# Two changes of where loads are issued: later keys, values and queries on GpSimd's queue, and the first queries ahead of the key-value products

## The chip, the cores and the metric

The kernel runs on one core of one Trainium2 chip. The metric is the device time of one execution in microseconds (us). Three runs of the kernel before took 1547.57, 1551.84 and 1552.95 us; their median, 1551.84 us, is the time before.

A core has five engines with a queue of instructions each: PE (TensorE, matrix products and transposes), DVE (VectorE), ACT (ScalarE), POOL (GpSimd) and SP (SyncE). Each works through its own queue strictly in order. An instruction that waits for a semaphore holds up everything behind it on that engine. Transfers between the memory of the chip and the core's on-chip memory (DMAs) are issued from such a queue too, and then run on 16 DMA engines which all queues share.

## The reference

```python
def _attn_ref(q, k, v, g_norm):                 # 8 batches, 8 heads, 576 positions, 64 wide
    kv = np.einsum('bhsd,bhse->bhde', k, v)
    out = np.einsum('bhsd,bhde->bhse', q, kv)
    rms = np.sqrt(np.mean(out * out, axis=-1, keepdims=True) + 1e-06)
    return out / rms * g_norm

x = attn_out.transpose(0, 2, 1, 3).reshape(4608, 512)
h = x @ w_in1;  g = h * np.clip(h + 3.0, 0.0, 6.0) / 6.0;  x = g @ w_out1     # layer 0: 512 -> 2048 -> 512
h = x @ w_in2;  g = h * np.cos(h);                          y = g @ w_out2     # layer 1: 512 -> 2048 -> 512
```

The attention is linear: each head needs a 64x64 product of keys and values, and then every query row is multiplied by it and normalised. The weights arrive in 8-byte numbers; the kernel decodes them itself.

## The kernel before, in words

The 4608 rows are worked on in nine superblocks of 512 rows, of four chunks of 128 rows each. There are three stages.

The prologue computes the four attention chunks of superblock 0. Batch 0's keys and values come in four pairs of heads: `kv_load` (L380) fetches one pair, `kv_pair` (L393) multiplies keys by values on PE (ten products, the last two on the 64 left-over positions in the tile `tail`), and DVE copies the result into `kvbd`. `q_load` (L419) fetches the queries of a chunk; `chunk` (L426) turns them on PE (`pq`), ACT copies them (`qT` or `tmp`), PE multiplies them by `kvbd` (`po`), ACT and DVE normalise, PE turns the result back (`px`) and ACT writes it to `xr`.

Then superblock 0 goes through layer 0 in float32: for each of 16 blocks `f`, `plain_1` (product `h`, L1012) and `plain_2` (product `acc`, L1027). This stage needs the decoded weights `di` and `do` of block pair `f // 2`. A weight is fetched by `raw_load` (L200, tiles `ri` and `ro`, 1024 KB each) into one of three raw buffers, decoded by ACT (L245, and L258 for a sum of squares) and DVE (L247, L251, L254). A raw buffer is free again after L258.

The remaining superblocks of layer 0 (products at L835 and L654) and all of layer 1 (L835 and L707) run as float16 products. During layer 0 a generator, `attention`, works off the other attention chunks between those products: for each batch four `kv_pair`s, and chunks in between. There is a single buffer, `kv_buf`, for the keys and values of the later batches: the load of a pair can start only when PE has done the products of the pair before it, and the next `kv_pair` stands in PE's queue at a place that is fixed when the program is built.

All loads and stores of the kernel before are issued from SP's queue, in the order in which the scheduler places them. What fixes the order on PE, DVE and ACT is the scheduler that builds the program; it follows the order of the Python code, with priorities, and its own expectation of when data arrive.

The steps touched are `kv_load` and `q_load`, the loads ahead of the prologue (L924 to L943) and the order of the prologue's work (L944 to L954).

Of the kernel before, what the change touches and what calls it, by code (L numbers as in the profile page):

```python
# [55 lines left out]
def attention_moe_kernel(  # L56
# [12 lines left out]
    nc = tc.nc  # L69
# [6 lines left out]
    NP = H // 2  # L76
# [32 lines left out]
    def col(n=1, p=P):  # L109
        c = next_col[0]  # L110
        next_col[0] = c + n
        return cols[0:p, c:c + n]
# [3 lines left out]
    kv_buf = const.tile([P, 2, 2, 5, D], F32, name="kv_buf")  # L116
# [26 lines left out]
    def ps_scratch(name):  # L143
        tag = scratch[turn_of[0] % len(scratch)]
        turn_of[0] += 1
        return ps_m.tile([P, 512], F32, tag=tag, name=name, bufs=2 if tag == "t" else 1)


    def pow2_scale(mx, name, squares, res, at=None):


        pt = ps_scratch(f"pt_{name}")
        nc.tensor.transpose(out=pt[0:1, 0:P], in_=mx, identity=ident)
        m1 = col(p=1)
        nc.vector.tensor_reduce(
            out=m1, in_=pt[0:1, 0:P], axis=AX.X, op=ALU.max, apply_absolute_value=True
        )
        yield
        pb = ps_scratch(f"pb_{name}")
        nc.tensor.matmul(out=pb[:, 0:1], lhsT=ones_row, rhs=m1, start=True, stop=True)  # L160
        t = sm_p.tile([P, 1], F32, tag="sc", name=f"t_{name}")
        lo, hi = (2.0 ** -96, 2.0 ** 96) if squares else (2.0 ** -48, 2.0 ** 48)
        nc.vector.tensor_scalar(out=t, in0=pb[:, 0:1], scalar1=hi, scalar2=lo, op0=ALU.min, op1=ALU.max)
        pw = sm_p.tile([P, 1], U32, tag="pw", name=f"pw_{name}")
        if squares:
            nc.vector.tensor_scalar(
                out=pw, in0=t.bitcast(U32), scalar1=1, scalar2=0x3F800000,
                op0=ALU.logical_shift_right, op1=ALU.bitwise_and,
            )
        else:  # L170
            nc.vector.tensor_scalar(
                out=pw, in0=t.bitcast(U32), scalar1=0x7F800000, scalar2=None, op0=ALU.bitwise_and
            )
        s, inv = at or (col(), col())
        nc.vector.tensor_scalar(out=inv, in0=pw.bitcast(F32), scalar1=(2.0 ** 63 if squares else 1.0) / TOP, scalar2=None, op0=ALU.mult)
        nc.vector.reciprocal(out=s, in_=inv)
        res[name] = (s, inv)
        yield

    def tiny(name, a, b=None, imm=None):  # L180
        t = col()
        if b is not None:
            nc.vector.tensor_tensor(out=t, in0=a, in1=b, op=ALU.mult)
            a = t
        if imm is not None:
            nc.vector.tensor_scalar(out=t, in0=a, scalar1=imm, scalar2=None, op0=ALU.mult)
        return t
# [6 lines left out]
    scale = {}  # L194
# [182 lines left out]

    def kv_load(b, p, t=kv_buf, tail=True):  # L380
        for n, src in enumerate((k, v)):
            nc.sync.dma_start(
                out=t[:, n, :, 0:4, :].rearrange("p h c d -> p h (c d)"),
                in_=src[b, 2 * p:2 * p + 2, 0:512, :].rearrange("h (p c) d -> p h (c d)", c=4),
            )
            if tail:
                nc.sync.dma_start(
                    out=t[0:64, n, :, 4, :],
                    in_=src[b, 2 * p:2 * p + 2, 512:576, :].rearrange("h p d -> p h d"),
                )  # L390
        return t

    def kv_pair(b, p, t, tail=None):  # L393
        ps = ps_scratch(f"kv{b}_{p}")
        for c in range(5):
            for h in range(2):
                if c == 4 and tail is not None:
                    kh, vh = (tail[:, m, 2 * p + h] for m in range(2))
                else:
                    kh, vh = (t[:, m, h, c, :] for m in range(2))  # L400
                nc.tensor.matmul(
                    out=ps[64 * h:64 * h + 64, 0:64], lhsT=kh, rhs=vh, start=(c == 0), stop=(c == 4)
                )
        for h in range(2):
            r = slice(64 * h, 64 * h + 64)
            nc.vector.tensor_copy(out=kvbd[r, b % 2, p, r], in_=ps[r, 0:64])
        yield

    def parts(c):

        r, res = 0, []
        while r < P:
            b, s = divmod(c * P + r, S)
            n = min(P - r, S - s)
            res.append((b, s, r, n))
            r += n
        return res

    def q_load(c, t=None):  # L419
        if t is None:  # L420
            t = at_p.tile([P, H, D], F32, tag="q", name=f"q{c}")
        for b, s, r, n in parts(c):
            nc.sync.dma_start(out=t[r:r + n], in_=q[b, :, s:s + n, :].rearrange("h p d -> p h d"))
        return t

    def chunk(c, qt, dst, after=None, tmp=None):  # L426
# [451 lines left out]
    def run(gen):  # L878
        for _ in gen:
            pass  # L880

    def g_scale():
        yield from pow2_scale(gn, "g", False, scale)
        nc.vector.tensor_scalar(
            out=gs, in0=gn, scalar1=scale["g"][0], scalar2=0.125, op0=ALU.mult, op1=ALU.mult
        )
        yield
# [34 lines left out]
    kv_t = {}  # L922
    q_t = {}
    tail = wi_p.tile([P, 2, H, D], F32, tag="wi", name="tail")  # L924
    nc.gpsimd.memset(tail[64:P], 0.0)
    nc.gpsimd.memset(kv_buf[64:P, :, :, 4, :], 0.0)
    kv_t[0, 0] = kv_load(0, 0, tail=False)
    for n, src in enumerate((k, v)):
        nc.sync.dma_start(out=tail[0:64, n], in_=src[0, :, 512:576, :].rearrange("h p d -> p h d"))
    for p in range(1, NP):  # L930
        t = wi_p.tile([P, 2, 2, 5, D], F32, tag="wi", name=f"kvs{p}")
        kv_t[0, p] = kv_load(0, p, t, tail=False)
    for c in range(2):
        q_t[c] = q_load(c)
    free["s"] -= 2
    xr0 = [s_p.tile([P, 2, TT], F32, tag="s", name=f"xr0_{n}") for n in range(2)]
    start(weights())
# [2 lines left out]
    nc.sync.dma_start(out=gn[64:128, :], in_=g_norm.rearrange("(p o) -> p o", o=1))  # L940
    qs = wi_p.tile([P, 2, H, D], F32, tag="wi", name="qs")
    for c in range(2):
        q_t[2 + c] = q_load(2 + c, qs[:, c])  # L943
    for p in range(NP):  # L944
        run(kv_pair(0, p, kv_t.pop((0, p)), tail))
    run(g_scale())
    isx = tiny("isx", scale["g"][1], imm=8.0)
    pro = [
        chunk(
            c, q_t.pop(c), [(2 * n, xr0[n][:, :, c * P:(c + 1) * P]) for n in range(2)],  # L950
# [1 line left out]
        )  # L952
        for c in range(4)
    ]  # L954
    n = 0
    while pro:
        for g in list(pro):
# [19 lines left out]
    def attention():  # L977

        n_kv, n_task = NP, 0
        kv_t[kvs[n_kv]] = kv_load(*kvs[n_kv])  # L980
        for c in (4, 5):
            q_t[c] = q_load(c)
        for c in range(4, NC):
            while n_kv < len(kvs) and kvs[n_kv][0] <= parts(c)[-1][0]:
                yield from until(ATT0 + n_task * ATTR)
                yield from kv_pair(*kvs[n_kv], kv_t.pop(kvs[n_kv]))
                n_kv, n_task = n_kv + 1, n_task + 1
                if n_kv < len(kvs):
                    kv_t[kvs[n_kv]] = kv_load(*kvs[n_kv])
            yield from until(ATT0 + n_task * ATTR)  # L990
            j, n = divmod(c, 4)
            if n == 0:
                yield from take("raw")
                xr = raw_p.tile([P, KD, TT], F32, tag="raw", name=f"x{j}")

            def after(c=c):
                if c + 2 < NC:
                    q_t[c + 2] = q_load(c + 2)

            yield from take("at")  # L1000
            start(run_chunk(c, xr, after))
            yield
            n_task += 1
# [91 lines left out]
    n = NG * (NSB - 2)  # L1095
# [36 lines left out]
```

## Time and profile before

| | |
|---|---|
| median of three runs | 1551.84 us |
| the profiled execution, its time | 1551.0 us |
| its span, first to last instruction | 1549.1 us |
| PE busy | 1516.1 us (98%) |
| DVE busy | 1226.3 us (79%) |
| ACT busy | 1052.3 us (68%) |
| POOL busy | 2.0 us |
| mean granted TensorE clock | 0.998 of full speed |
| bytes moved by SP's DMA queue | 178.28 MB |

The profile lists, for each engine, how long it was busy in a stretch of time. TensorE's clock has two levels, 1.2 and 2.4 GHz; a granted clock of 1.00 means 2.4 GHz and 0.50 means 1.2 GHz. A timeline row gives the start, the length, the engine and line, output and input tiles, and in square brackets the idle time of the engine before it with what ended it. The chain of waits is followed back from the last instruction: each row names what the next one waited for. Of a DMA, the row's time is from its issue until the data had landed. SPq is SP's queue.

### The profile page before, as it was taken

What the parts mean: (1) busy time and instruction counts of PE and PEld (TensorE: products, weight loads), DVE (VectorE), ACT (ScalarE), POOL (GpSimd) and SP (SyncE); (2) the same over time, 40 slices, a digit from 0 to 9 for tenths busy, and PEclk for the clock granted to TensorE, in tenths of its full rate; (3) what the DMA queues carried; (4) which work ended last, traced back from release to release, by engine and by line L of the source; (5) the groups of instructions that cost most, each with busy time, mean ns of one, the idle gap of its engine ahead of it and who ended that gap; (6) DMA issues with size and microseconds to landing.
All of it is one profiled execution on the core that took longest, in us unless ns stands there. A gap on an engine that the chain in (4) does not pass through costs nothing.

```text
span 1549.1 us, 28806 instructions
## 1 busy us (share of the span) xinstructions
PE 1516.1 (98%) x11902; PEld 1153.8 (74%) x11902; DVE 1226.3 (79%) x2234; ACT 1052.3 (68%) x1714; POOL 2.0 (0%) x8
## 2 busy tenths in 40 slices
PE   6999999999999999999999999999999999999998
PEld 6444676666667676766666678888888888888887
DVE  4899877786877687876475799989898989889881
ACT  4567665665666565665455788888888887878771
POOL 0000000000000000000000000000000000000000
PEclk9999999999999999999999999999999999999999
DMA  7653433325243342402031233343342424333434
GB/s 205 202 165 95 123 102 110 103 81 165 69 150 98 88 129 74 150 25 79 1 103 48 96 110 117 129 142 116 139 142 105 157 91 155 117 132 123 147 111 155
DMA packets 112067, 180.12 MB, mean 116 GB/s; under 512 B 51008, under 2 KB 83776, under 8 KB 102720
## 3 DMA queue, kind: packets, MB, share of 16 engines
q1 hardware_dynamic: 111936, 178.28, 34.9%
q8 instruction: 93, 1.52, 0.4%
q14 instruction: 38, 0.31, 0.1%
HBM read 144.70 MB, written 33.55 MB: 115 GB/s over the span
## 4 chain that ended last, share of the span: by engine, by line
PE 51%; DVE 31%; ACT 12%; DMA 3%; issue 2%; SPq 1%; ACTq 0%
PE acc L654 18%; PE P L835 10%; DVE uA L587 5%; PE R L835 5%; DVE uA L592 4%; DVE gs_A L264 4%; DVE gs_S L264 4%; ACT uA L589 3%; PE h L1012 3%; PE Q L835 3%; PE acc L1027 3%; DVE c L851 2%; ACT uA L590 2%; PE po L449 2%; PE P L707 2%
## 5 line engine op out<-in xcount | busy, mean ns | idle before, releaser
L835 PEld LDWEIGHTS <-wi 128*128 128x128 f16 x5712 | 557.3, 98 | 108.7 <-issue 5.1
L654 PE MATMUL acc<-g,wo 128*128 128x512 f16 x1536 | 368.9, 379 | 0.4 <-ACT g L561 0.3
L654 PEld LDWEIGHTS <-wo 128*128 128x128 f16 x1536 | 148.8, 98 | 135.0 <-issue 1.7
L835 PE MATMUL P<-xoB,wi 128*128 128x256 f16 x1536 | 190.3, 273 | 1.6 <-ACT sn L847 1.5
L835 PE MATMUL P<-xoT,wi 128*128 128x256 f16 x1536 | 189.1, 273 | 0.5 <-ACT sn L847 0.2
L707 PEld LDWEIGHTS <-gs_A 128*128 128x128 f16 x1632 | 159.7, 98 | 20.4 <-issue 1.9
L847 ACT ACTIVATE sn<-P 128x512 f32<-128x512 f32 x204 | 119.2, 584 | 63.3 <-PE P L835 62.7
L707 PEld LDWEIGHTS <-gs_S 128*128 128x128 f16 x1392 | 136.1, 98 | 22.0 <-issue 6.2
L589 ACT ACTIVATE uA<-uA,cols 128x512 f32<-128x512 f32 x144 | 103.6, 720 | 62.3 <-DVE uA L587 60.9
L548 ACT ACTIVATE u<-c,cols 128x512 f32<-128x512 f32 x96 | 77.9, 812 | 82.2 <-DVE c L851 62.3
L707 PE MATMUL P<-wo,gs_S 128*128 128x256 f16 x888 | 114.6, 273 | 5.0 <-ACT kv_buf L726 5.0
L563 DVE TENSOR_TENSOR g<-u,g 128x512 f16<-128x512 f32 x128 | 87.5, 687 | 30.1 <-ACT g L561 29.1
L707 PE MATMUL P<-wo,gs_A 128*128 128x256 f16 x840 | 107.2, 273 | 1.6 <-ACT kv_buf L726 1.6
L561 ACT ACTIVATE g<-u 128x512 f16<-128x512 f32 x128 | 80.1, 628 | 37.5 <-DVE u L550 36.9
L550 DVE SCALAR_TENSOR_TENSOR u<-u,cols,c 128x512 f32<-128x512 f32 x96 | 71.9, 749 | 39.7 <-ACT u L548 39.4
L262 ACT ACTIVATE gs_A<-uA,cols 128x512 f16<-128x512 f32 x125 | 88.3, 713 | 16.2 <-DVE uA L592 11.3
L264 DVE SCALAR_TENSOR_TENSOR gs_A<-uA,cols,gs_A 128x512 f16<-128x512 f32 x125 | 92.6, 746 | 7.1 <-ACT gs_A L262 5.1
L585 ACT ACTIVATE uA<-c,cols 128x512 int32<-128x512 f32 x108 | 77.2, 715 | 30.0 <-DVE c L856 21.8
L835 PE MATMUL R<-xoT,wi 128*128 128x256 f16 x768 | 94.7, 273 | 0.0
L835 PE MATMUL Q<-xoB,wi 128*128 128x256 f16 x768 | 94.6, 273 | 0.0
L835 PE MATMUL R<-xoN,wi 128*128 128x256 f16 x768 | 94.5, 273 | 0.0
L592 DVE SCALAR_TENSOR_TENSOR uA<-uA,c 128x512 f32<-128x512 f32 x108 | 74.1, 686 | 23.0 <-ACT uA L590 22.1
(205 smaller groups left out, 2242.4 us busy)
## 6 DMA issues: line engine op xcount, KB each, us to landing
wo<-wod SPq DMA_DIRECT2D x63, 1024.0 KB, 4.9
ri<-in_moe_w_in_dram SPq DMA_DIRECT2D x16, 1024.0 KB, 6.5
ro<-in_moe_w_out_dram SPq DMA_DIRECT2D x16, 1024.0 KB, 5.1
x2d<-o SPq DMA_DIRECT2D x36, 256.0 KB, 2.5
xr<-x2d SPq DMA_DIRECT2D x9, 1024.0 KB, 4.8
out_dram<-o SPq DMA_DIRECT2D x36, 256.0 KB, 4.0
q<-in_q_dram SPq DMA_DIRECT2D x30, 256.0 KB, 2.9
kv_buf<-in_k_dram SPq DMA_DIRECT2D x29, 256.0 KB, 2.9
```

The source lines that it names most:

```text
L262: nc.scalar.activation(out=hi, in_=src, func=AF.Copy, scale=s)
L264: nc.vector.scalar_tensor_tensor(out=lo, in0=src, scalar=s, in1=hi, op0=ALU.mult, op1=ALU.subtract)
L548: nc.scalar.activation(out=u, in_=c, func=AF.Relu, scale=u0[:, gi:gi + 1], bias=b0[:, gi:gi + 1])
L561: nc.scalar.activation(out=gt[:, :, 0, sl], in_=u, func=AF.Copy)
L563: nc.vector.tensor_tensor(out=gt[:, :, 1, sl], in0=u, in1=gt[:, :, 0, sl], op=ALU.subtract)
L587: stt(out=u, in0=ui, scalar=nk, in1=c, op0=ALU.mult, op1=ALU.add)
L589: nc.scalar.activation(out=u, in_=u, func=AF.Sin, scale=hf)
L592: stt(out=u, in0=u, scalar=0.5 * SIG2, in1=c, op0=ALU.subtract, op1=ALU.mult)
L654: nc.tensor.matmul(out=acc[e], lhsT=w[:, a, row, e * P:(e + 1) * P], rhs=g[:, c], start=(n == 0 and i == 0), stop=(n == NF - 1 and i == 2),)
L707: nc.tensor.matmul(out=ps[:, mt], lhsT=g[:, c, pr, mt * P:(mt + 1) * P], rhs=w[:, i, a], start=(first and k == 0), stop=(end and k == 2), ...
L835: nc.tensor.matmul(out=ps[bank][:, pr], lhsT=w[:, a, A_AT[an], kk], rhs=x[:, c, kk], start=(first and pr == 0 and i == 0 and kk == 0), sto ...
L847: nc.scalar.activation(out=sn[n], in_=ps["P"], func=AF.Copy)
```

## The change

`kv_load` and `q_load` take the engine that issues their DMAs; without one it is GpSimd. The loads of the prologue (batch 0's keys and values, chunks 0 to 3's queries) name SP, so they stay on SP's queue. All later loads of keys, values and queries move to GpSimd's. Then the queries of chunks 0 and 1 are issued ahead of all keys and values, and the two generators that start chunks 0 and 1 are stepped once (the turn `pq` and the copy `tmp`) before the key-value products are written down.

```diff
-    def kv_load(b, p, t=kv_buf, tail=True):
+    def kv_load(b, p, t=kv_buf, tail=True, eng=None):
+        eng = eng or nc.gpsimd
         for n, src in enumerate((k, v)):
-            nc.sync.dma_start(
+            eng.dma_start(
...
-    def q_load(c, t=None):
+    def q_load(c, t=None, eng=None):
...
-            nc.sync.dma_start(out=t[r:r + n], in_=q[b, :, s:s + n, :].rearrange("h p d -> p h d"))
+            (eng or nc.gpsimd).dma_start(out=t[r:r + n], in_=q[b, :, s:s + n, :].rearrange("h p d -> p h d"))
...
-    kv_t[0, 0] = kv_load(0, 0, tail=False)
+    for c in range(2):
+        q_t[c] = q_load(c, eng=nc.sync)
+    kv_t[0, 0] = kv_load(0, 0, tail=False, eng=nc.sync)
...
-        kv_t[0, p] = kv_load(0, p, t, tail=False)
-    for c in range(2):
-        q_t[c] = q_load(c)
+        kv_t[0, p] = kv_load(0, p, t, tail=False, eng=nc.sync)
...
-        q_t[2 + c] = q_load(2 + c, qs[:, c])
-    for p in range(NP):
-        run(kv_pair(0, p, kv_t.pop((0, p)), tail))
-    run(g_scale())
-    isx = tiny("isx", scale["g"][1], imm=8.0)
+        q_t[2 + c] = q_load(2 + c, qs[:, c], nc.sync)
     pro = [
...
+    for g in pro[:2]:
+        next(g)
+    for p in range(NP):
+        run(kv_pair(0, p, kv_t.pop((0, p)), tail))
+    run(g_scale())
+    isx = tiny("isx", scale["g"][1], imm=8.0)
```

On SP's queue, the first place is right behind the first `ro` load of the prologue. `ri_0`, `ro_0` and `ri_1`, `ro_1` are the first two pairs of layer 0's weights; `kv_buf` rows are loads of batch 1's first two pairs, and `q_366`, `q_369` are chunks 4 and 5's queries. Before:

```order
17 L208 DMA ro_0_360<-in_moe_w_out_dram 128x2x1024
18 L382 DMA kv_buf<-in_k_dram 128x2x256
19 L387 DMA kv_buf<-in_k_dram 64x2x64
20 L382 DMA kv_buf<-in_v_dram 128x2x256
21 L387 DMA kv_buf<-in_v_dram 64x2x64
22 L423 DMA q_366<-in_q_dram 64x8x64 x2
23 L423 DMA q_369<-in_q_dram 128x8x64
24 L382 DMA kv_buf<-in_k_dram 128x2x256
25 L387 DMA kv_buf<-in_k_dram 64x2x64
26 L382 DMA kv_buf<-in_v_dram 128x2x256
27 L387 DMA kv_buf<-in_v_dram 64x2x64
28 L208 DMA ri_1_394<-in_moe_w_in_dram 128x4x512
```

The same stretch of SP's queue now, with the semaphores that each row waits for:

```order
13 L208 DMA ri_0_149<-in_moe_w_in_dram 128x4x512 [waits DMAHW4_49]
14 L940 DMA cols<-in_g_norm_dram 64x1 [waits DMAHW5_49]
15 L941 DMA cols<-in_g_norm_dram 64x1 [waits DMAHW6_49]
16 L424 DMA qs<-in_q_dram 128x8x64 [waits DMAHW7_49]
17 L424 DMA qs<-in_q_dram 128x8x64 [waits DMAHW0_49]
18 L208 DMA ro_0_360<-in_moe_w_out_dram 128x2x1024 [waits DMAHW1_49]
19 L208 DMA ri_1_394<-in_moe_w_in_dram 128x4x512 [waits DMAHW2_49]
20 L208 DMA ro_1_422<-in_moe_w_out_dram 128x2x1024 [waits DMAHW4_49,DMAHW3_49,Activation_49]
```

Eleven loads that stood between `ro_0` and `ri_1`, four of which wait for PE's products of batch 1's first pair, are gone from SP's queue.

On POOL's queue, whose only work was to fill tiles at the start, those loads now stand right behind that work, with these waits:

```order
10 L927 MEMSET kv_buf 64x4x64 [waits Pool_49]
11 L383 DMA kv_buf<-in_k_dram 128x2x256 [waits DMAHW2_49,PE_49]
12 L388 DMA kv_buf<-in_k_dram 64x2x64
13 L383 DMA kv_buf<-in_v_dram 128x2x256 [waits DMAHW3_49]
14 L388 DMA kv_buf<-in_v_dram 64x2x64
15 L424 DMA q_366<-in_q_dram 64x8x64 [waits DMAHW0_49,PE_49]
16 L424 DMA q_366<-in_q_dram 64x8x64
17 L424 DMA q_369<-in_q_dram 128x8x64 [waits DMAHW1_49,PE_49]
18 L383 DMA kv_buf<-in_k_dram 128x2x256 [waits DMASW0_49,PE_49]
```

The first of them waits only for the first loads of `kv_buf` and for the first eight products of batch 0; the queries wait for the turns of chunks 0 and 1.

On ACT the decode of the second pair of weights moves ahead of the work of blocks 0 and 1. Now:

```order
29 L482 ACTIVATE xr0_1_148<-px3_349,cols_116 128x2x128
30 L245 ACTIVATE di0_1_416<-ri0_1_394 128x1024
31 L245 ACTIVATE do0_1_444<-ro0_1_422 128x1024
32 L258 ACTIVATE ro0_0_360,cols_116<-do0_0_384 128x1024
33 L1021 ACTIVATE u0_0_413<-h0_0_396,cols_116 128x512
34 L1021 ACTIVATE u0_1_441<-h0_1_424,cols_116 128x512
```

Rows 30 and 31 stood behind row 34 before.

## Rows read from the trace of the kernel before

**Rows 1.** The page's first part: busy time, share of span, instructions.
```profile
PE 1516.1 (98%) x11902; PEld 1153.8 (74%) x11902; DVE 1226.3 (79%) x2234; ACT 1052.3 (68%) x1714; POOL 2.0 (0%) x8
```

**Rows 2.** Busy time in stretches: stretch, length, each engine, clock, DMA share, GB/s.
```profile
0.00:10.00 10.00, 2.95 (x40) 2.47 (x40) 1.75 (x6) 1.49 (x2) 1.97 (x8) 1.00 0.76 228
10.00:20.00 10.00, 8.43 (x71) 7.34 (x71) 3.15 (x11) 4.28 (x7) 0.00 (x0) 1.00 1.00 277
20.00:30.00 10.00, 6.31 (x37) 5.58 (x38) 8.71 (x35) 7.43 (x17) 0.00 (x0) 0.84 0.53 159
...
150.00:170.00 20.00, 19.20 (x126) 11.80 (x126) 19.92 (x45) 15.73 (x26) 0.00 (x0) 1.00 0.31 96
170.00:190.00 20.00, 18.68 (x172) 13.26 (x168) 16.06 (x31) 11.31 (x16) 0.00 (x0) 1.00 0.50 143
```

**Rows 3.** PE's timeline at the third block's first product.
```profile
46.88 5.37 PE L1012 MATMUL h<-xr,di 128*128 128x512 f32 x8 [2.25 <-DVE di L254]
```

**Rows 4.** The chain of waits, 31 to 74 us: start, length, what.
```profile
31.96 0.27 SPq L382
...
34.27 8.06 DMA ri<-in_moe_w_in_dram
42.35 1.14 ACT di L245
...
69.82 3.43 PE h L1012 x8
```

**Rows 5.** Stretches around PE's two idle times, columns as in rows 2.
```profile
24.00:26.00 2.00, 0.00 (x0) 0.00 (x0) 1.66 (x9) 1.83 (x4) 0.00 (x0) 1.00 0.67 150
...
28.00:29.00 1.00, 1.00 (x6) 1.00 (x6) 0.93 (x4) 0.80 (x3) 0.00 (x0) 0.50 0.00 0
...
48.00:49.00 1.00, 1.00 (x2) 0.34 (x1) 1.00 (x2) 1.00 (x1) 0.00 (x0) 0.50 0.00 0
```

**Rows 6.** The chain of waits in the prologue.
```profile
8.80 7.97 DMA ri<-in_moe_w_in_dram
16.80 1.15 ACT di L245
```

**Rows 7.** PE's timeline: the first key-value products.
```profile
4.42 1.12 PE L401 MATMUL kv<-kv_buf 128*64 128x64 f32 x16 [4.42 <-DMA kv_buf<-in_v_dram]
```

**Rows 8.** ACT's timeline: the instruction that frees the first raw buffer.
```profile
24.68 1.06 ACT L258 ACTIVATE ri<-di 128x1024 f32<-128x1024 f32 x1
```

**Rows 9.** PE's timeline around batch 2's key-value products.
```profile
163.70 0.80 PE L401 MATMUL kv<-kv_buf 128*64 128x64 f32 x20
...
168.16 0.27 PE L153 MATMUL pt_x<-ident,cols 128*1 128x128 f32 x1 [0.49 <-DVE cols L775]
...
169.49 0.80 PE L401 MATMUL kv<-kv_buf 128*64 128x64 f32 x20 [0.30 <-DMA kv_buf<-in_v_dram]
...
173.25 1.47 PE L835 MATMUL P<-xoB,wi 128*128 128x256 f16 x12 [0.69 <-ACT sn L847]
175.35 0.80 PE L401 MATMUL kv<-kv_buf 128*64 128x64 f32 x20 [0.63 <-DMA kv_buf<-in_v_dram]
...
182.86 0.80 PE L401 MATMUL kv<-kv_buf 128*64 128x64 f32 x20
```

**Rows 10.** The chain of waits: the load that ends the second wait.
```profile
172.13 3.08 DMA kv_buf<-in_v_dram
```

**Rows 11.** POOL's longest instruction, on its timeline.
```profile
1.00 0.95 POOL L925 MEMSET tail<- 64x1024 f32 x1
```

**Rows 12.** SP's queue: the longest issue of a left-over load in the prologue.
```profile
17.73 1.39 SPq L387 DMA_DIRECT2D kv_buf<-in_k_dram  x1
```

**Rows 13.** PE's timeline: two key-value products of batch 3, and layer 0's longest idle time.
```profile
244.94 0.80 PE L401 MATMUL kv<-kv_buf 128*64 128x64 f32 x20
254.24 0.80 PE L401 MATMUL kv<-kv_buf 128*64 128x64 f32 x20
...
270.34 0.38 PE L160 MATMUL pb_o<-cols,ones_row 1*128 1x1 f32 x2 [1.77 <-DVE cols L155]
```

More of the change, by code (lines that the diff above doesn't have):

```diff
@@ L386, in kv_load @@
             if tail:
-                nc.sync.dma_start(
+                eng.dma_start(
                     out=t[0:64, n, :, 4, :],
```

## The prediction

> **What bounds the kernel now.** I read the page's busy times first, then the busy time in stretches, then PE's timeline wherever PE was not full, and the chain of waits there. PE is busy for 1516.1 of 1549.1 us [rows 1], so all that any change of loads can win is in the 33 us in which PE stands still, and in stretches at the lower clock. In the stretches the reader is to see where those lie [rows 2]: 7.05 us in the first 10 us, 1.57 in the next ten, 3.69 in the third, and, much later, 0.80 and 1.32 us in the two stretches of 20 us in which batch 2's keys and values are multiplied. One more is on PE's timeline: 2.25 us ahead of the third block's product at 46.88 [rows 3]. Layer 1, more than half of the span, has no attention in it and none of the instructions that change.
>
> At the gap before 46.88 the chain of waits shows what ended last [rows 4]: weight `ri_1` was issued only at 34.27, because it stands in SP's queue behind the load of batch 1's second pair. That load needs `kv_buf`, which PE gave back only shortly before 31.96. The weight takes 8.06 us to land, then ACT and DVE decode it. When PE goes on it is slower: the granted clock is 0.50 (1.2 GHz) in the stretch from 48 to 49 us, and the same had happened from 28 to 29 us, after PE had stood still from 24 to 26 us [rows 5]. Eight `h` products then took 5.37 us [rows 3] where the same eight take 3.43 us later [rows 4].
>
> In the prologue the chain runs through `ri_0`: issued at 8.80, landed at 16.80, decoded by ACT at once [rows 6]. ACT's and DVE's decode of `ri_0` stand in their queues ahead of the evictions and sums of the attention chunks, before and after the change, so everything up to the first `h` is timed from that landing. DMA share is 1.00 from 10 to 20 us, at 277 GB/s [rows 2].
>
> **The change part by part.**
>
> *The gap at 46.88 goes.* `ri_1` now stands directly behind `ro_0` on SP's queue and has a free raw buffer, so it is issued as soon as `ro_0` is. `ro_1` needs the buffer that ACT's L258 frees at 24.68 + 1.06 = 25.74 [rows 8], well ahead of its use. The decode then stands right behind the last `xr` eviction. PE saves the idle 2.25 us and the slow clock's 5.37 - 3.43 = 1.94 us: -4.2 us. What is late next: in ACT's new order the decode of `do_1` stands ahead of `u0_0`, which PE waits for. `ri_1` took 8.06 us with other loads beside it [rows 4]; if `ro_1` takes as long it lands at about 34 us, when ACT gets to it. A few us more would cost PE about 1 us. I put 0, with 0 to 1 as bounds.
>
> *The prologue is held up.* Batch 1's first pair (256 + 32 + 256 + 32 KB) and chunk 4's queries (256 KB) stood behind `ro_0` in one queue. On POOL's they need only the first products and turns on PE: 4.42 + 1.12 [rows 7] and 1.9 us for the queries that now go first (512 KB at 277 GB/s), so from about 7.5 us, while `kvs`, `ri_0`, `qs` and `ro_0` are still to come on SP's queue. All of it goes through the same DMA engines, which are full. 832 KB at 277 GB/s is 3.1 us; chunk 5's 256 KB as well would make it 4.0, and if POOL's packets yielded to SP's it would be 0. I take 3.1: +3.1 us on `ri_0` and all behind it. The Trainium skill, "DMA: Bandwidth & Descriptors", section "Issuing engines are not separate DMA queues", says that DMAs run on the same 16 engines and interleave whichever engine started them, and that a second issuer only saves issue time. By that rule it is 3.1, and without it 0; the full share above agrees, but no row of this kernel has two queues at work.
>
> *The first queries ahead of the keys.* SP issues the same bytes ahead of `ri_0` in another order, so `ri_0` does not land sooner by it. The two turns and their two ACT copies go under the wait for keys and values. ACT had time for them in the trace too, since it starts the decode the moment that `ri_0` lands [rows 6]. I put 0. The key-value products come later by the same 1.9 us; `ri_0`'s landing covers that, and without the cover up to 1.9 would show.
>
> *Keys and values on POOL's queue in layer 0.* PE's place for each pair is fixed and `kv_buf` is single, so what counts is the time T from the end of one pair's products to the landing of the next pair. On SP's queue it was 172.13 + 3.08 - (169.49 + 0.80) = 4.9 us [rows 9, 10]. No row shows a DMA issued by POOL. From below, T stays 4.9. From above: four loads one after another at 1.39 us, the longest issue of such a load [rows 12], and the landing: 3 x 1.39 + 3.08 = 7.25 us. The nearest row on the engine itself is POOL's longest instruction, 0.95 us [rows 11]; with it T = 3 x 0.95 + 3.08 = 5.9 us, which I take. A sentence apart: the same page of the Trainium skill, table "Specifications", gives a first-byte latency of about 1 us for GpSimd's path and 0.6 for SP's; as an estimate that is 0.4 us for each of four loads in turn, T = 6.5 and 1.2 us more below.
>
> PE's other work between batch 2's first and second pair is 169.49 - 163.70 less 0.80 for the products and 0.49 and 0.30 of idle: 4.20 us; between second and third 5.86 - 0.80 - 0.69 - 0.63 = 3.74 [rows 9]. With T = 5.9 PE idles 1.7 and 2.2 us, 3.9 in place of the 2.1 that these two intervals idle now: +1.8. The third interval has 182.86 - 175.35 - 0.80 = 6.7 us of work and hides it. At T = 7.25 it is 3.05 + 3.5 + 0.55 - 2.1 = +5.0. Idles of this length may cost the clock too: 2.25 us was followed by 1.2 GHz [rows 3, 5], while no loss showed after 1.77 us [rows 13]. Each such fall is 1.9 us; I put none, and two (3.8) in the bound. In the later batches pairs are 254.24 - 244.94 = 9.3 us apart [rows 13], which leaves 8.5 us: hidden at any T up to there. Query loads have two chunks' time and are hidden. SP's other loads and stores lose the rows that stood in front of them; nothing on PE waited for those, so 0.
>
> *Sum.* 1551.0 (the profiled execution) - 4.2 + 3.1 + 1.8 = 1551.7. The median of the runs shown is 0.84 above the profiled execution, so 1552.5 us.
>
> **The rivals.**
>
> *POOL issues slowly (slower).* If POOL needs 1.39 us or more for each load, or has to wait for something it shares, T is 7.25 or more: -4.2 + 3.1 + 5.0 + 3.8 of clock = +7.7, about 1559.5 us. From T = 8.5 on it decides everything, since then 15 more intervals in batches 3 to 7 are exposed: at T = 10 these alone are 15 x 1.5 = 22 us, a time near 1590. For it: the chain is single-buffered and already waited for data on SP's queue twice [rows 9]. Against it: 15 of the 18 intervals of batches 2 to 7 have 8.5 us. DVE is busy for 19.92 of 20 us where the tight intervals lie [rows 2]. The Trainium skill, "SBUF — State Buffer", section "Who interferes with whom", says that GpSimd shares a pair of ports with DVE, and that it cannot write the descriptors of its DMAs while DVE works in a two-port mode. By that rule this rival is the likelier one the busier DVE is; no row of before shows POOL beside a busy DVE.
>
> *POOL's loads cost nothing (faster).* POOL starts late enough, or its packets are few enough in the full prologue, that `ri_0` lands as before, and T stays near 4.9. Then the 4.2 us stay won, and the weights decoded earlier can also take away the 0.49 and 0.69 us for which PE waited on DVE and ACT and part of 1.77 [rows 9, 13]: -4.2 to -7, about 1546.5. For it: DVE was busy for 19.92 of 20 us from 150 to 170 [rows 2], so earlier decoding could help there. Against it: the waits of the first POOL loads are over by about 7.5 us.
>
> *The gap is not removed.* `ri_1` is early, but `ro_1` or a later weight gates the in-order ACT queue, so PE stops at about the same place: +3.1 + 1.8 = about 1556.7. Against it: the raw buffers come free in time by the rows above.
>
> **How the numbers follow.** A change within 0.3% (4.7 us) is about what a measurement of this kernel can't tell from none. Forecast (gain and new waits nearly cancel) 0.46; POOL slow 0.30; POOL free 0.19; gap stays 0.05. Faster 0.20: nearly all of the free case, and a little of the forecast. Same 0.46. Slower 0.34. The likeliest case's own range, with 0 to 4.0 for the prologue, T up to 7.25 without the clock, is 1547.5 to 1557. The range that takes in the free case and the slow one up to T = 8.5 (4.0 in the prologue, 4.3 + 4.8 + 1.8 - 2.1 of idle, 3.8 of clock: 1564) is 1545 to 1565.
>
> **What would show it.** Right: PE's timeline has no idle of 2 us ahead of the third block's `h` and no 1.2 GHz stretch behind it; `ri_0` lands near 20 us in place of 16.8 and the first `h` starts about 3 us later; batch 2's second and third pairs wait about 2 us each for `kv_buf`; later batches wait for nothing. Wrong: `ri_0` lands by 17.5; POOL's queue shows issues of far over 1 us; PE waits for `kv_buf` in batches 3 to 7; a difference in layer 1.

## The result and the profile after

The changed kernel takes 1561.22 us (median of 4 runs, 1559.78 to 1563.57); the kernel before took 1550.63 in the runs beside it (4 runs, 1547.57 to 1552.95). The ratio is 1.0076, 95% interval 1.006 to 1.0091: slower, where the forecast was that no difference could be measured. The time lies in the range that was given, but outside the likeliest case's own. The profiled execution took 1561.49 us with a span of 1559.7 us, 10.6 us longer than before. A table of stages below shows where they lie in these two executions.

The page's busy times, queues (packets, MB, share of the 16 DMA engines' time) and DMA issues of the changed kernel (the issue rows end with size and median us to landing):

```profile
PE 1520.3 (97%) x11902; PEld 1156.7 (74%) x11902; DVE 1228.1 (79%) x2234; ACT 1053.2 (68%) x1714; POOL 105.9 (7%) x156
...
q1 hardware_dynamic: 55296, 153.37, 28.3%
q0 software_dynamic: 8896, 24.91, 5.5%
...
kv_buf<-in_k_dram POOLq DMA_DIRECT2D x28, 256.0 KB, 3.1
kv_buf<-in_v_dram POOLq DMA_DIRECT2D x28, 256.0 KB, 3.5
```

The same of the kernel before, where these loads were SP's:

```profile
q1 hardware_dynamic: 111936, 178.28, 34.9%
...
kv_buf<-in_k_dram SPq DMA_DIRECT2D x29, 256.0 KB, 2.9
kv_buf<-in_v_dram SPq DMA_DIRECT2D x29, 256.0 KB, 3.2
```

PE is busy 4.2 us longer than before [rows 1] with the same 11902 instructions: part of the loss is clock, the rest idle time. PE's timeline (start, length; in brackets idle time ahead and its releaser) shows both. `pt_g` is a small turn that belongs to the scale of `g_norm`, and `pb_o` and, further on, `pb_i` are small products that spread a weight's scale over the partitions. `o` is the tile in which a quarter of a superblock's result of layer 0 is stored to the array `x2d` in the chip's memory:

```profile
7.13 1.12 PE L402 MATMUL kv<-kv_buf 128*64 128x64 f32 x16 [7.13 <-DMA kv_buf<-in_v_dram]
...
19.72 0.27 PE L153 MATMUL pt_g<-ident,cols 128*1 128x128 f32 x1 [4.35 <-DMA cols<-in_g_norm_dram]
...
35.86 6.74 PE L1015 MATMUL h<-xr,di 128*128 128x128 f32 x58
42.44 3.60 PE L1030 MATMUL acc<-u,do 128*128 128x512 f32 x8
45.88 3.60 PE L1015 MATMUL h<-xr,di 128*128 128x512 f32 x8
...
163.19 0.80 PE L402 MATMUL kv<-kv_buf 128*64 128x64 f32 x20
...
172.06 1.33 PE L402 MATMUL kv<-kv_buf 128*64 128x64 f32 x20 [3.71 <-DMA kv_buf<-in_v_dram]
...
179.85 0.80 PE L402 MATMUL kv<-kv_buf 128*64 128x64 f32 x20
...
187.36 0.80 PE L402 MATMUL kv<-kv_buf 128*64 128x64 f32 x20
...
274.96 0.38 PE L160 MATMUL pb_o<-cols,ones_row 1*128 1x1 f32 x2 [1.88 <-DVE cols L155]
...
374.48 1.02 PE L655 MATMUL acc<-g,wo 128*128 128x512 f16 x3 [2.42 <-ACT o L668]
```

The gap ahead of the third block's `h` is gone, and the same eight products take 3.60 us where they took 5.37 [rows 3]. In return PE stands still in three other places: 4.35 us for the small load of `g_norm`, 3.71 us for batch 2's second pair (`kv2_1` in what follows), where it had waited 0.30 [rows 9], and 2.42 us at 374.48, where the kernel before shows no idle time at all. Behind each of them the granted clock falls (stretch, length, PE busy, clock, DMA share, GB/s):

```profile
20.00:24.00 4.00, 2.58 (x11) 0.50 0.98 351
...
172.00:176.00 4.00, 3.94 (x32) 0.50 0.45 149
276.00:280.00 4.00, 4.00 (x12) 0.58 0.13 50
374.00:378.00 4.00, 3.52 (x16) 0.62 0.19 71
```

The fourth, from 276 us, follows the 1.88 us wait of `pb_o`; the kernel before waited 1.77 us there [rows 13] and kept its clock. In the prologue the chain of waits shows the weight's landing at 19.29 in place of 16.80 [rows 6]:

```profile
8.12 11.15 DMA ri<-in_moe_w_in_dram
19.29 1.13 ACT di L245
```

POOL's own issues are short, also beside a busy DVE (2.92 of 3.00 us from 164 to 167). On POOL's timeline:

```profile
8.56 0.84 POOL L383 DMA_DIRECT2D kv_buf<-in_k_dram  x1 [5.86 <-PE kv L402]
...
164.18 0.70 POOL L383 DMA_DIRECT2D kv_buf<-in_k_dram  x1 [8.81 <-PE kv L402]
164.88 0.61 POOL L388 DMA_DIRECT2D kv_buf<-in_k_dram  x1
165.48 0.71 POOL L383 DMA_DIRECT2D kv_buf<-in_v_dram  x1
166.19 0.61 POOL L388 DMA_DIRECT2D kv_buf<-in_v_dram  x1
```

SP's queue shows what now runs beside them: a weight of 1 MB at 166.00 and another at 365.70, between two stores of `o`:

```profile
166.00 0.38 SPq L208 DMA_DIRECT2D ri<-in_moe_w_in_dram  x1
...
364.92 0.34 SPq L670 DMA_DIRECT2D x2d<-o  x1
365.70 0.38 SPq L208 DMA_DIRECT2D ro<-in_moe_w_out_dram  x1
366.96 0.32 SPq L670 DMA_DIRECT2D x2d<-o  x1
```

Before, that first weight was issued at 173.39, behind the loads of two pairs.

Cut at six instructions of PE that stand in the same order in every kernel here, each profiled execution gives a table of stages (us, from starts on PE's timeline):

| kernel | to first 58 `h` | to batch 2's first pair | to its fourth | to `pb_o` | to `pb_i` | to next `pb_o` | to end |
|---|---|---|---|---|---|---|---|
| before | 31.87 | 131.83 | 19.16 | 87.48 | 70.74 | 70.03 | 1137.99 |
| after | 35.86 | 127.33 | 24.17 | 87.60 | 72.27 | 74.04 | 1138.43 |
| difference | +4.0 | -4.5 | +5.0 | +0.1 | +1.5 | +4.0 | +0.4 |

The rounded differences add up to 10.5 of the 10.6 us. They are those of single executions: below, kernels whose prologues are the same differ by up to 1.5 us in the first stage.

### The profile page after: what moved, and what is told of

Read it like the earlier page. It is cut to its first block, busy times and chain, and to the rows that moved or that the text cites. A ratio compares the mean times of both kernels' runs of the same rounds, so it can differ in the third digit from the quotient of the medians.

```text
span 1559.7 us, 28841 instructions
## 1 busy us (share of the span) xinstructions
PE 1520.3 (97%) x11902; PEld 1156.7 (74%) x11902; DVE 1228.1 (79%) x2234; ACT 1053.2 (68%) x1714; POOL 105.9 (7%) x156
## 3 DMA queue, kind: packets, MB, share of 16 engines
q1 hardware_dynamic: 55296, 153.37, 28.3%
q0 software_dynamic: 8896, 24.91, 5.5%
## 4 chain that ended last, share of the span: by engine, by line
PE 46%; DVE 30%; ACT 12%; issue 8%; DMA 3%; POOL 1%; SPq 0%; POOLq 0%; ACTq 0%
PE acc L655 17%; PE P L836 10%; DVE uA L588 5%; PE R L836 5%; DVE uA L593 4%; DVE gs_A L264 4%; DVE gs_S L264 4%; ACT uA L590 3%; PE Q L836 3%; DVE c L852 2%; ACT uA L591 2%; PE h L1015 2%; PE P L708 2%; ACT gs_A L262 2%; PE acc L1030 2%
```

## The experiments

Three theories. T1, collision: SP's one queue had kept big weight loads away from transfers that PE or ACT waits for; with two queues they meet on the shared DMA engines, and each wait costs clock as well. T2: POOL's path is slow in itself. T3: the order with the queries first costs the time. Ratios below are against runs of the kernel before on the same chip, taken beside them.

**Each half of the change alone.** Only the loads moved, prologue order as before (all later batches' keys and values, and chunks from 4 on, on POOL):

```
+        eng = nc.sync if b == 0 else nc.gpsimd
...
-            nc.sync.dma_start(out=t[r:r + n], in_=q[b, :, s:s + n, :].rearrange("h p d -> p h d"))
+            (nc.sync if c < 4 else nc.gpsimd).dma_start(out=t[r:r + n], in_=q[b, :, s:s + n, :].rearrange("h p d -> p h d"))
```

> The kernel before with its order of the prologue, but with the later batches' keys, values and queries loaded by POOL. Three theories of the 10.6 us that the change lost. T1, collision: loads that no longer stand in one line on SP's queue run beside critical transfers: POOL's early loads beside ri_0 (+4.0 us), layer 1's weight ri_1 beside batch 2's keys and values (+5.0), ro_3 between the x2d stores (about +4), and the gap at the third block goes (-4.5). T2, POOL's path is slow in itself: its transfers take longer whatever runs beside them. T3, the queries-first order costs it. T1 and T2 expect 1559 to 1562 us here with the same three waits (kv2_1 on PE 3 to 4 us, o on PE near 374 us over 2 us, h of the first projection 3 to 4 us later than before); T3 expects about 1546 us, none of these.

Measured: 1558.47 us, ratio 1.0046 (1.0033 to 1.0058), half a microsecond under what T1 and T2 had. `kv2_1` waits 3.57 us, `o` lets PE wait 2.2 us, and the first 58 `h` begin at 35.58. And only the order, every load on SP:

```
-        eng = eng or nc.gpsimd
+        eng = eng or nc.sync
...
-            (eng or nc.gpsimd).dma_start(out=t[r:r + n], in_=q[b, :, s:s + n, :].rearrange("h p d -> p h d"))
+            (eng or nc.sync).dma_start(out=t[r:r + n], in_=q[b, :, s:s + n, :].rearrange("h p d -> p h d"))
```

> The changed kernel's order (first queries loaded and turned ahead of the key-value products) with every load on SP. T1 and T2 expect that order alone neither gains nor loses: the wait on di of about 2.25 us at the third block stays, kv2_1 waits under 0.5 us, no wait over 2 us for o near 374 us: 1549 to 1553 us. T3 expects the loss here: about 1560 us.

Measured: 1548.51 us, ratio 0.9988 (0.9978 to 0.9997). T3 falls: the loss comes with the loads on POOL, waits and all, and the order alone is, if anything, a little faster. Its time is half a microsecond under what T1 and T2 had. PE's timeline of the order alone:

```profile
47.35 3.24 PE L1015 MATMUL h<-xr,di 128*128 128x512 f32 x7 [1.68 <-DVE di L254]
```

The gap stays, 0.6 us shorter. The loads alone ended 2.3 us of span earlier than the full change; 1.7 of it lie in the stage after `pb_o` (70.58 in place of 72.27), where the wait was 1.61 us and the clock stayed at 1.00.

**One pair alone.** The kernel before, with only batch 1's second pair on POOL, the load behind which `ri_1` had stood:

```
+        eng = nc.gpsimd if (b, p) == (1, 1) else nc.sync
```

> The kernel before with one edit: batch 1's second pair of keys and values alone is loaded by POOL; every other load and the order stay. T1 expects the gain without the collisions: ri_1 is issued two megabytes earlier, the wait on di at the third block (2.25 us and the slow clock behind it) goes, POOL's pair is wanted 100 us later and collides with nothing that is waited for at once: about 1550.6 - 4.2 = 1546.4 us (1545 to 1548). T2 expects ri_1 to be held up by POOL's transfer, the gap or a wait of kv1_1 in its place: 1550 us or more.

Measured: 1547.43 us, ratio 0.9978 (0.9969 to 0.9988). It came as T1 had it. Its first products run through without an idle time:

```profile
31.37 6.74 PE L1013 MATMUL h<-xr,di 128*128 128x128 f32 x58
37.95 4.46 PE L1028 MATMUL acc<-u,do 128*128 128x512 f32 x10
42.24 3.60 PE L1013 MATMUL h<-xr,di 128*128 128x512 f32 x8
```

The second stage takes 127.32 us, as in the full change: those 4.5 us are won by this one pair. Its ratio is the lowest of all, a gain of 0.22% (3.4 us), though the interval overlaps with that of the order alone. In this execution, too, `pb_o` waited long (1.95 us) and the stage behind it took 72.18 us.

**One collision taken away at a time.** Batch 1's first pair and chunk 4's and 5's queries back on SP:

```
-        kv_t[kvs[n_kv]] = kv_load(*kvs[n_kv])
+        kv_t[kvs[n_kv]] = kv_load(*kvs[n_kv], eng=nc.sync)
-            q_t[c] = q_load(c)
+            q_t[c] = q_load(c, eng=nc.sync)
```

> The changed kernel, but batch 1's first pair of keys and values and the queries of chunks 4 and 5 (832 KB, which POOL loaded beside the first weight) stand on SP again behind the first weight's first pieces. T1 (collision): h of the first projection begins 2.5 to 4 us earlier than the 35.86 us of the changed kernel, the wait of pt_g on g_norm falls from 4.35 us to under 1 us, the gap at the third block stays away because the second pair is still POOL's; the waits of kv2_1 and of o stay: about 1561.2 - 4 = 1557 us. A rival, T4 (the queries-first order makes the prologue late): h of the first projection still begins after 35 us, 1560 us or more.

Measured: 1557.91 us, ratio 1.005 (1.0037 to 1.0064). The edit moves 1088 KB: the pair's 576 and 256 for each of the two chunks; the 832 leave out chunk 5's.

```profile
15.75 0.27 PE L153 MATMUL pt_g<-ident,cols 128*1 128x128 f32 x1 [0.71 <-DMA cols<-in_g_norm_dram]
...
32.77 6.74 PE L1015 MATMUL h<-xr,di 128*128 128x128 f32 x58
```

The order with the queries first is still in it, and `h` begins 3.1 us earlier than at 35.86: the delay came with POOL's early loads. It is beyond the scatter: the four kernels with the changed kernel's prologue have their first 58 `h` at 35.86 to 37.16 us, the three with that order and SP's loads at 32.10 to 32.91. Next, batch 2's pairs back on SP:

```
-        eng = eng or nc.gpsimd
+        eng = eng or (nc.sync if b == 2 else nc.gpsimd)
```

> The changed kernel, but batch 2's four pairs of keys and values are loaded by SP, so that layer 1's first weight ri_1 stands behind them again. T1: the wait of kv2_1 falls from 3.71 us to under 0.5 us and the clock of 160 to 180 us rises from 0.83 to near 1; the prologue's loss and the wait of o stay: about 1561.2 - 5 = 1556 us. If ri_1 was not the cause (x2d's stores alone, or PE's later place), the wait stays over 2 us and the time within 2 us of the changed kernel's.

Measured: 1555.88 us, ratio 1.0042 (1.0029 to 1.0055); the third stage takes 19.15 us, as before the change.

```profile
170.15 0.80 PE L402 MATMUL kv<-kv_buf 128*64 128x64 f32 x20 [0.20 <-DMA kv_buf<-in_v_dram]
```

That moves both POOL and the weight. To part them, the pairs stay with POOL and layer 1's raw weights go there too, behind the pairs:

```
-        nc.sync.dma_start(out=dst, in_=src)
+        (nc.gpsimd if layer else nc.sync).dma_start(out=dst, in_=src)
```

> The changed kernel with one edit: layer 1's raw weights are issued by POOL too, so that ri_1 of layer 1 stands behind batch 2's keys and values in one line again, and ro_3 no longer stands between the x2d stores on SP. T1 expects the 3.71 us wait of kv2_1 on PE to fall under 1 us and the 2.42 us wait near 374 us to go, at about 1561.2 - 5 - 4 = 1552 us, with the prologue's +4.0 left. T2 expects kv2_1 to wait 3 us or more still, since its own loads go the same way, and the weights to come later as well: 1559 us or more.

Measured: 1555.35 us, ratio 1.0029 (1.002 to 1.0038).

```profile
170.96 0.80 PE L402 MATMUL kv<-kv_buf 128*64 128x64 f32 x20 [1.66 <-DMA kv_buf<-in_v_dram]
```

The wait falls from 3.71 to 1.66 us, not under 1 as T1 had it, and not over 3 as T2 had it; the time, too, lies between theirs. The wait for `o` is gone as T1 had it. The load of values that ends it, issued from 163 to 168 us, lands in 6.4 us in the changed kernel, in 4.4 here and in 3.3 with the batch on SP; of each, the issue's row with size and us to landing, first the changed kernel, then this one, then the one with batch 2 on SP:

```profile
kv_buf<-in_v_dram POOLq DMA_DIRECT2D x1, 256.0 KB, 6.4
```

```profile
kv_buf<-in_v_dram POOLq DMA_DIRECT2D x1, 256.0 KB, 4.4
```

```profile
kv_buf<-in_v_dram SPq DMA_DIRECT2D x1, 256.0 KB, 3.3
```

So the weight beside it is worth 2.0 us and POOL's side about 1. Whether that 1 us is POOL's path, or that all four stores of `o` now go ahead of the pair's values (on SP the fourth is issued behind them), was not parted. Over all 28 pairs the medians to landing, shown above, are 3.1 and 3.5 us from POOL and 2.9 and 3.2 from SP.

Last, layer 1's one weight `ro_3` taken from between the stores:

```
-        nc.sync.dma_start(out=dst, in_=src)
+        (nc.gpsimd if (layer, kind, i) == (1, "o", 3) else nc.sync).dma_start(out=dst, in_=src)
```

> The changed kernel, but layer 1's one weight ro_3 (1 MB) is issued by POOL, so that it no longer stands between the x2d stores on SP. T1: the wait for o near 374 us falls from 2.42 us to under 0.5 us, the clock of 300 to 400 us rises from 0.98 to 1.00, everything ahead stays: about 1561.2 - 4 = 1557 us. If the megabyte delays the stores on the shared engines whichever queue it is in, the wait stays over 1.5 us and the time at 1560 us or more.

Measured: 1556.1 us, ratio 1.0042 (1.003 to 1.0054). The wait is gone, and the stage from `pb_i` to the next `pb_o` takes 69.80 us in place of 74.04.

**All three together.**

> The changed kernel with the three edits together: first loads of batch 1 and of chunks 4 and 5 on SP, batch 2's pairs on SP, ro_3 on POOL; all other later loads stay POOL's and the queries-first order stays. If the three collisions are the whole loss (T1), the three gains add: 1561.2 - 4 - 5 - 4 = 1548 us (1546 to 1550), at or below the kernel before. If something else about POOL's loads costs (T2), it stays at 1553 us or more.

Measured: 1548.41 us, ratio 0.9993 (0.9984 to 1.0001). Taken by the ratios, the three single edits win 0.26, 0.34 and 0.34%, which is 0.94; together they win 0.83. Within the intervals, the three collisions are the loss. All keys and values of batches 3 to 7 are still POOL's in it. They begin in the stage to `pb_o`, which takes 87.22 us here and 87.48 before, and end in the last, which takes 1138.80 us; in all eleven kernels the last took 1137.8 to 1138.9. So T2 has no more room than the 1 us above.

**The same loads, the kernel before's prologue order.** The kernel before with the edit to `ro_3` shown above, and with:

```
+        eng = nc.sync if b in (0, 2) or (b, p) == (1, 0) else nc.gpsimd
...
+            (nc.sync if c < 6 else nc.gpsimd).dma_start(out=t[r:r + n], in_=q[b, :, s:s + n, :].rearrange("h p d -> p h d"))
```

> The loads as in the run with the three edits together (first loads of batch 1 and of chunks 4 and 5 and batch 2's pairs on SP, layer 1's ro_3 and all other later loads on POOL), but with the kernel before's order of the prologue. T1: the gap is gone, no collision, and the prologue as in the kernel before: 1546 to 1549 us, the same as with one pair alone on POOL (1547.4), so that POOL's loads in the long middle are worth nothing either way. If the queries-first order is worth something of its own, this is 1 us or more slower than the three edits with that order (1548.4); if POOL's later loads gain, it is under 1546 us.

Measured: 1550.14 us, ratio 0.9998 (0.9988 to 1.0007). T1 had expected a gain of some 3 us, and there is none: this corrects T1. `ro_3` is on POOL here too, and yet ACT and PE wait again at the same place. ACT's timeline:

```profile
363.52 0.69 ACT L668 ACTIVATE o<-acc,cols 128x512 f32<-128x512 f32 x1 [3.21 <-DMA x2d<-o]
```

The issues explain it. POOL's `ro_3` and SP's second store on their timelines, and then the store's row among the DMA issues (KB, us to landing), in this kernel:

```profile
356.40 0.72 POOL L208 DMA_DIRECT2D ro<-in_moe_w_out_dram  x1 [7.20 <-DVE kvbd L407]
...
357.17 0.32 SPq L670 DMA_DIRECT2D x2d<-o  x1
```

```profile
x2d<-o SPq DMA_DIRECT2D x1, 256.0 KB, 6.2
```

and in the kernel with only `ro_3` on POOL:

```profile
366.44 0.71 POOL L208 DMA_DIRECT2D ro<-in_moe_w_out_dram  x1 [7.43 <-DMA x2d<-o]
...
366.67 0.32 SPq L670 DMA_DIRECT2D x2d<-o  x1
```

```profile
x2d<-o SPq DMA_DIRECT2D x1, 256.0 KB, 2.8
```

The issue of POOL's `ro_3` is over at 357.12 in the one, before the store's begins at 357.17; in the other it is over at 367.15, after the store's, which is over at 366.99. In the changed kernel it began 1.26 us ahead of the store, on SP's own queue, and the store landed in 6.7 us. So in these rows it does not matter which queue carries the megabyte, but whether it is issued ahead of the second store, and that is decided by less than a microsecond. The kernel before has such a late store too: there `ro_3` stands behind the third, and the fourth lands in 6.0 us, but nothing waits for it. The stage is 73.61 us long, 3.7 more than with the three edits in the other order. So the comparison of the two prologue orders that this run was to make stays open.

## Why the prediction came out as it did

| term of the sum | predicted | measured | |
|---|---|---|---|
| gap at the third block | -4.2 | -4.5 | right, shown by one pair alone |
| prologue | +3.1 | +4.0 | right mechanism; too few bytes, order and clock left out |
| batch 2's pairs | +1.8 | +5.0 | wrong cause, too small |
| SP's other loads and stores | 0 | +4.0 | failed |
| clock after `pb_o` | 0 | +1.5 | failed |
| rest | 0 | +0.5 | |

**The gap** went as argued. None of the waits behind it that were feared came.

**The prologue.** `ri_0` landed 2.5 us later, for 3.1 predicted, and the figure is near because two errors went against each other. ACT starts the decode when `ri_0` has landed; its rows with the order alone, with the early loads back on SP, and with the loads alone:

```profile
15.37 1.13 ACT L245 ACTIVATE di<-ri 128x1024 f32<-128x1024 f32 x1 [5.17 <-DMA ri<-in_moe_w_in_dram]
```

```profile
15.25 1.14 ACT L245 ACTIVATE di<-ri 128x1024 f32<-128x1024 f32 x1 [5.01 <-DMA ri<-in_moe_w_in_dram]
```

```profile
17.74 1.13 ACT L245 ACTIVATE di<-ri 128x1024 f32<-128x1024 f32 x1 [1.60 <-DMA ri<-in_moe_w_in_dram]
```

The new order, put at 0, lets `ri_0` land 1.4 us sooner than before (16.80 [rows 6]). POOL's early loads then bring it from 15.25 to 19.29: 4.0 us, which is the prediction's own figure for both chunks' queries. It had counted chunk 4's alone, and POOL had issued chunk 5's too by 13.58. The rule weighed in the prediction, that DMAs interleave whichever engine starts them (the Trainium skill, "DMA: Bandwidth & Descriptors", "Issuing engines are not separate DMA queues"), agrees with these 4.0 us and with the store that came late from either queue (6.7 and 6.2 us).

The other 1.5 us arise behind the landing. The prediction timed everything up to the first `h` from it; but from the landing to the 58 `h` it took 15.1 us before, 16.6 in the changed kernel, 17.5 with the order alone and 17.8 with the loads alone. The clock goes with that. From 22 to 24 us, before and with the loads alone (stretch, length, PE busy, clock, DMA share, GB/s):

```profile
22.00:24.00 2.00, 1.43 (x11) 1.00 0.95 261
```

```profile
22.00:24.00 2.00, 2.00 (x11) 0.50 1.02 407
```

In the changed kernel PE stood still for 4.35 us for the small load of `g_norm` (0.2 KB), issued right behind `ri_0`, and ran what followed at 0.50. That wait is not needed for a late prologue: with the loads alone it was 0.33 us and `ri_0` landed only 0.9 us later than before, and `h` still began 3.7 us later: 2.8 of that lie behind the landing, with the clock at 0.50 from 22 to 34 us. Why it fell in that execution, where PE's idle times ahead of it were 1.1 us at most, stays open.

**Batch 2's pairs.** T was to be 4.9 to 7.25 us, from the time that POOL needs to issue. It was 172.06 - (163.19 + 0.80) = 8.1. The issues took 0.61 to 0.71 us, less than the 0.95 assumed; what grew was the landing, put at 3.08 us and measured at 6.4; of that, 2.0 us were layer 1's `ri_1`, issued at 166.00 beside it. Of the 5.0 us of the stage 3.1 lie in this interval (8.87 us in place of 5.79). The next one, put at 2.2 us of idle time, waited for no load, but took 7.79 us in place of 5.86, 1.9 more, with the clock at 0.50 from 172 to 176 us.

**The step that failed** is the sentence "SP's other loads and stores lose the rows that stood in front of them; nothing on PE waited for those, so 0". It asked who waits for SP's remaining transfers, and not what they meet when they start earlier. Two of the losses come from there: layer 1's `ri_1` no longer stands behind batch 2's loads, and `ro_3` comes between two stores of `o`, whose two buffers ACT needs back. The second is the more instructive, since neither transfer was touched by the change. That no fall of the clock was counted is a second error: the bound of 3.8 us was named and then left out of the sum, though each of the three new waits was followed by a fall.

That the time lies in the range is luck in the main: its upper part stood for a slow POOL. This rival, "POOL issues slowly", came nearest in time (1559.5) with the wrong mechanism: POOL's 0.61 to 0.85 us are far from the 1.39 from which it counted, and the waits in batches 3 to 7 that it needed are not there. The rule brought for it, that GpSimd cannot write descriptors beside DVE's two-port mode (the Trainium skill, "SBUF — State Buffer", "Who interferes with whom"), cost nothing visible here: the mean issue is 0.61 to 0.85 us over 148 issues, with DVE busy for 79% of the span. Whether DVE was in that mode beside them, no row shows.

## What to carry to other kernels

A queue with one line is also an order of priority: a load that waits in it for a buffer holds back the big transfers behind it, and these may be just the ones that must not run now. Before moving loads to a second queue, list what starts earlier on the first one, and lay its megabytes over the transfers that someone waits for with one or two buffers. Move only the load that blocks: here one pair of the 28 had the whole 4.5 us of the second stage, and in no other stage did a kernel gain more than 0.3 us from the rest. A wait that PE gets in return is to be priced with the slower clock behind it: of the 5.0 us of batch 2's pairs, 1.9 lay in an interval without a wait.

## What was not expected of the hardware

- Between 353 and 375 us, in the eleven kernels, a 256 KB store of `o` issued 0.5 to 4.0 us behind a weight of 1 MB, on the same queue or on another, landed in 4.7 to 9.6 us. The others landed in 2.0 to 3.7 us, and one in 5.0.
- The 24.91 MB that moved to POOL's queue went in 8896 packets there. On SP's they had been 111936 - 55296 = 56640, and yet SP's share of the engines' time fell only from 34.9 to 28.3%, with 5.5% for POOL's.
- POOL needed 0.71 us to issue a 256 KB load of keys and 0.61 us for its 32 KB tail; the cost goes with the instruction more than with the bytes.
- The wait of `pb_o` varies with what precedes it. In the kernels here in which it was 1.29 to 1.66 us, the 70 us that follow took 70.6 to 70.9; with 1.75, 1.85, 1.88 and 1.95 us they took 72.2 to 72.3, though 1.77 in the kernel before still gave 70.74. A wait of this size is worth 1.5 us more or nothing.
- Prologues that are the same differ from execution to execution: the changed kernel's began its first 58 `h` at 35.86, 36.81, 37.14 and 37.16 us, the kernel before's at 31.37, 31.87 and 32.91. Differences of 1.5 us in that stage between two single executions show nothing.
